# A recurrent layer with an ELU feed-forward block: the moment of the bank copies, the steps of the output sums, and the order of the last products

## The chip, the cores and the metric

The kernel runs on one core of a Trainium2 chip. The metric is the device time in microseconds (us) of one execution. The core's engines are named as in the profile: PE multiplies matrices (PEld are its weight loads), DVE, ACT and POOL work on vectors, SP issues transfers. PE writes to PSUM, which has eight banks here; DVE and ACT read PSUM and SBUF, POOL reads and writes SBUF alone.

## What is computed

The reference is a gated linear recurrence over 768 tokens for 4 x 8 heads of size 48, whose output goes through a feed-forward block with an ELU:

```python
f = 1.0 / (1.0 + np.exp(-f_logit))
for t in range(S):
    state = f[:, :, t, :, None] * state + np.einsum('bhd,bhe->bhde', k[:, :, t], v[:, :, t])
    y[:, :, t] = np.einsum('bhd,bhde->bhe', q[:, :, t], state)
...
h = x @ w_in
g = np.where(h > 0.0, h, alpha * (np.exp(np.minimum(h, 0.0)) - 1.0))
return (g @ w_out).astype(np.float32)
```

x has 3072 tokens of 384 numbers, w_in is 384 x 2048, w_out is 2048 x 384, all in fp32.

## The kernel before

The 3072 tokens are 12 units of 256. The program is one list written out by hand (`manual_schedule`): each engine does its instructions in the order in which the loop at L1263 emits them, so an instruction that waits holds up all that stands behind it on its engine. The loop runs over 16 half steps T for each unit. At an even T it emits the up-projection of one pair P, 256 of the 2048 hidden columns (`up`, for units from 1 on `up7`). At an odd T it emits the joins of that pair (`joined`), whatever `plan` has for this T, and the down-projection of an earlier pair (`down(P - LAG)`, two pairs behind). A unit has eight pairs, called P0 to P7 here.

Both projections save products by sums, as Strassen's method does. In `up7` (L946) PE makes four products in one PSUM bank (`pa`); ACT copies one of them to `u` (L963); DVE adds it to others (L965, `hh`); then `elu` of the pair before is emitted, and PE makes six products in a second bank (`pb`). In `joined` (L975) DVE adds the second bank's products to the first's in three instructions (L978), and ACT applies Relu and Exp (L988, L989). The two banks of tag `h` are taken in turn: the `pa` of a pair has to wait for L965 of the pair before, its `pb` for L978 of the pair before. `elu` (L1007) finishes the activation on DVE (L1010). After an even pair POOL makes four sums of hidden columns (SUMS_OF_TWO), after an odd one DVE makes three (SUMS_SOON) and POOL eight (SUMS_OF_FOUR).

In `down` two pairs, a quad, make 20 products of 128 x 128 x 128 (PRODUCTS, ten for the even pair and ten for the odd), each a row such as "x4 b10 c0": hidden column block or sum, weight block or combination of weights, target. The 16 targets c0 to c15 lie four to a bank in the banks m3, m0, m1 and m2, in this order; all four quads of a unit add into them. After the unit's last product `ended` (L1092) is called at once: ACT copies three banks to SBUF (`kept`, L1097) and c15 to a piece of `spare` (L1099), and the 22 output sums (OUTPUTS) with the stores go on a list, `pending`. c12 to c14 are read straight from PSUM, in the first three sums. Each half step takes four items off that list (SPREAD). The last product of a unit is emitted at step 3 of the next (T%16 = 3), so the list is empty after step 8.

Other work around this. At step 2 of a unit the keys of the next are transposed (PE and ACT). At step 5 `both` makes its state products (banks a0, a1) and its scores (banks m3 and m0 of the products), which DVE masks and adds up; at this step there is no down-projection, and step 7 has two. At steps 9 and 11 its outputs and the carried part follow. At steps 9, 11, 13 and 15 the decays of the unit after that are made: a scan (L680) and a reciprocal (L685) on DVE for three of them, products on POOL (L675). At step 13 POOL makes differences of x for the next unit (`blend`, L944). Weights are read again to be checked by ACT at steps 2, 6, 10 and 14 (L658, L659).

In the last unit the even pair of the last quad gives no products; all 20 are emitted together after the last up-projection, in the order of the banks, then the copies and OUTPUTS_AT_THE_END, of which POOL makes four sums and DVE 18.

```python
        if j == NP - 1:
            ended(m)
...
        for f in pending[:SPREAD]:
            f()
        del pending[:SPREAD]
```

Of the kernel before, what the change touches and what calls it, by code (L numbers as in the profile page):

```python
# [355 lines left out]
def table(text):  # L356
    return [tuple(row.split()) for row in text.split(",") if row.strip()]
# [6 lines left out]
    "a0 x0 - x1, a1 a0 - x4, a2 x5 + a1, a3 x0 - x4, "  # L364
)
SUMS_SOON = table(
    "a5 x2 - x6, a7 x4 + x2, a10 x2 - x7, "
)
SUMS_OF_FOUR = table(
    "a12 a0 + x7, a4 x6 - x7, a6 x5 + a4, a9 x4 + x6, a8 x1 + x2, a8 a8 - x3, a13 x0 + x2, a11 x3 - x7, "  # L370
)
COMBINATIONS = table(
    "b0 w3 - w4, b1 w0 + b0, b2 w1 - b1, b1 b1 - w2, b1 b1 - w10, b4 w11 + w8, b3 w7 - b2, b2 w10 _ b2, "
# [2 lines left out]
)  # L376
PRODUCTS = (
    table(
        "x4 b10 c0, x5 w5 c11, x1 b12 c14, a0 b1 c2, a1 b8 c1, a2 w3 c8, a3 b6 c7, x7 b9 c10, x2 b5 c4, "
        "a5 w6 c9, "  # L380
    ),
    table(
        "a7 b3 c3, a10 b4 c5, a12 b7 c6, a4 b13 c11, a6 b0 c15, a9 b11 c15, a8 w11 c14, a8 w10 c13, "
        "a13 b2 c13, a11 w9 c12, "
    ),
)
OUTPUTS = table(
    "o0 c7 + c12, o1 c3 - c13, o2 c7 - c14, c1 c0 + c1, c2 c2 - c1, c4 c3 - c4, c5 c5 + c4, c6 c6 - c2, "
    "c8 c8 - c6, c9 c9 - c5, o0 o0 + c10, o0 o0 + c5, o0 o0 - c6, o1 o1 + c7, o1 o1 + c2, o2 o2 + c4, "
    "o2 o2 - c1, o3 c10 + c8, o3 o3 - c9, o5 c11 - c0, o5 o5 - c9, o4 c8 - c15, "  # L390
)
OUTPUTS_AT_THE_END = table(
    "c1 c0 + c1, c2 c2 - c1, c4 c3 - c4, c5 c5 + c4, c6 c6 - c2, c8 c8 - c6, o0 c7 + c5, o1 c3 + c7, "
    "o2 c7 + c4, o5 c11 - c0, c9 c9 - c5, o3 c10 + c8, o0 o0 - c6, o1 o1 + c2, o2 o2 - c1, o5 o5 - c9, "
    "o3 o3 - c9, o0 o0 + c10, o2 o2 - c14, o1 o1 - c13, o4 c8 - c15, o0 o0 + c12, "
)


# [2 lines left out]
def fast(ctx: ExitStack, tc: tile.TileContext, q, k, v, f_logit, w_in, w_out, out, flag, outer):  # L401
# [18 lines left out]
    nc = tc.nc  # L420
# [9 lines left out]
    NU = B * UPB  # L430
# [4 lines left out]
    NP = NFT // 2  # L435
    DH = DM // 2
    NQ = NFT // 4
    DIRECT = 1
    PLAIN = 2
    SPREAD = 4  # L440
# [108 lines left out]
    spare = cst.tile([128, sum(sizes)], FP32, name="spare")  # L549
# [10 lines left out]
    wo = cst.tile([128, NFT, DM], FP32, name="wo")  # L560
# [414 lines left out]
    def joined(P):  # L975
        m, j = order[P]
        h, pb = phs[P]
        add = lambda to, x, y: nc.vector.tensor_tensor(out=to, in0=x, in1=y, op=ALU.add)  # L978
        u43 = sb.tile([128, 2, 128], FP32, tag="u43h", name=f"u43h{m}_{j}")
        add(u43[:], pb[:, 0::2], h[:, 0:1].broadcast_to([128, 2, 128]))  # L980
        add(h[:, 2:4], pb[:, 1::2], u43[:])
        add(h[:, 4], pb[:, 0], u43[:, 1])
        exped(P, h[:, 1:].rearrange("n (i t) f -> n i (t f)", i=2))
# [23 lines left out]
    def elu(P):  # L1007
        m, j = order[P]
        g = gs[P]
        nc.vector.scalar_tensor_tensor(  # L1010
            out=g[:], in0=g[:], scalar=-1.0, in1=phs.pop(P), op0=ALU.add, op1=ALU.max
        )
        if m < PLAIN:
            return
        Q = P // 2
        if P % 2 == 0:
            ss[Q] = sb.tile([128, 14, 128], FP32, tag="sums", name=f"sums{m}_{j // 2}")
        for engine, rows in ((nc.gpsimd, SUMS_OF_TWO),) if P % 2 == 0 else (
            (nc.vector, SUMS_SOON), (nc.gpsimd, SUMS_OF_FOUR)
        ):  # L1020
            for row in rows:
                combined(engine, lambda name: hidden(Q, name), row)

    def combined(engine, at, row):
        to, x, sign, y = row
        engine.tensor_tensor(out=at(to), in0=at(x), in1=at(y), op=ALU.add if sign == "+" else ALU.subtract)  # L1026

    def hidden(Q, name):
        i = int(name[1:])
        if name[0] == "a":  # L1030
            return ss[Q][:, i]
        t, f = divmod(i, 4)
        return gs[2 * Q + f // 2][:, f % 2, t * 128 : (t + 1) * 128]

    def weight(Q, name):
        i = int(name[1:])
        if name[0] == "b":
            return combos[i][:, Q]
        f, n = divmod(i, 3)
        return wo[:, 4 * Q + f, n * 128 : (n + 1) * 128]  # L1040

    left = []

    def down(P):
        m, j = order[P]
        if m < PLAIN:
            if j == 0:
                pms[m] = [
                    ps.tile([128, DM], FP32, tag=f"m{i}", name=f"psM{m}_{i}") for i in ((0, 3) if m else (1, 2))
                ]  # L1050
            pm, g = pms[m], gs.pop(P)
            for i in range(2):
                for t in range(NW):
                    nc.tensor.matmul(
                        pm[t][:], lhsT=g[:, i, t * 128 : (t + 1) * 128], rhs=wo[:, 2 * j + i, :],
                        start=(j == 0 and i == 0), stop=(j == NP - 1 and i == 1),
                    )
            if j == NP - 1:
                o = (outer if (NU - m) % 2 else sb).tile([128, 2, DM], FP32, tag="o", name=f"o{m}", bufs=1)
                for t in range(NW):  # L1060
                    nc.scalar.copy(o[:, t], pm[t][:])
                    t0 = m * U + t * 128
                    nc.sync.dma_start(out=out[t0 : t0 + 128, :], in_=o[:, t])
                del pms[m]
            return
        Q = P // 2
        if j == 0:
            pms[m] = [ps.tile([128, 4, 128], FP32, tag=f"m{i}", name=f"psM{m}_{i}") for i in (3, 0, 1, 2)]
            begun.clear()
        pm = pms[m]  # L1070
        whole = m == NU - 1 and j >= NP - 2
        if whole and j == NP - 2:
            return
        todo = PRODUCTS[j % 2]
        if whole:
            todo = sorted(PRODUCTS[0] + PRODUCTS[1], key=lambda row: int(row[2][1:]) // 4)
        for x, y, c in todo:
            bank, at = divmod(int(c[1:]), 4)
            nc.tensor.matmul(  # L1079
                pm[bank][:, at], lhsT=hidden(Q, x), rhs=weight(j // 2, y),  # L1080
                start=bank not in begun, stop=(j == NP - 1), skip_group_check=True,
            )
            begun.add(bank)
        if j % 2:
            gs.pop(P - 1), gs.pop(P), ss.pop(Q)
        if j == NP - 1:
            ended(m)

    begun = set()
    pending = []  # L1090

    def ended(m):  # L1092
        pm = pms.pop(m)
        o = (outer if (NU - m) % 2 else sb).tile([128, 2, DM], FP32, tag="o", name=f"o{m}", bufs=1)
        kept = sb.tile([128, 12, 128], FP32, tag="kept", name=f"kept{m}", bufs=1)
        for b in range(3):
            nc.scalar.copy(kept[:, 4 * b : 4 * b + 4], pm[b][:])  # L1097
        last = spare[:, NQ * 128 : (NQ + 1) * 128]
        nc.scalar.copy(last, pm[3][:, 3])  # L1099

        def at(name):
            i = int(name[1:])
            if name[0] == "o":
                return o[:, i // 3, i % 3 * 128 : (i % 3 + 1) * 128]
            return last if i == 15 else kept[:, i] if i < 12 else pm[3][:, i - 12]

        def store(*queues):
            for t in range(2):
                for h in ((1, 0) if t else (0, 1)):
                    queues[t].dma_start(  # L1110
                        out=out[m * U + t * 128 : m * U + (t + 1) * 128, h * DH : (h + 1) * DH],
                        in_=o[:, t, h * DH : (h + 1) * DH],
                    )

        if m < NU - 1:
            pending.extend(lambda row=row: combined(nc.vector, at, row) for row in OUTPUTS)
            pending.append(lambda: store(nc.sync, nc.sync))
            return
        for row in OUTPUTS_AT_THE_END:
            combined(nc.gpsimd if row[0] in ("o3", "o5") else nc.vector, at, row)  # L1120
        left.append(store)
# [141 lines left out]
    for T in range(NU * NFT):  # L1263
        P = T // 2
        sevens = order[P][0] >= DIRECT
        if T % 2 and sevens:
            joined(P)
        if T % 2 == 0 and P and order[P - 1][0] < DIRECT:
            elu(P - 1)
        for f in plan.pop(T, ()):  # L1270
            f()
        if T % 2 == 0:
            up(P)
        elif P >= LAG and T not in joint:
            if T - 2 in joint:
                down(P - LAG - 1)
            down(P - LAG)
        for n in later.pop(T, ()):
            split(n)
            if n not in (A1[2], A1[2] + 1):  # L1280
                lower(n)
        for f in pending[:SPREAD]:
            f()
        del pending[:SPREAD]
    elu(NU * NP - 1)
    for P in range(NU * NP - LAG, NU * NP):
        down(P)
# [50 lines left out]
```

## Time and profile before

| what | value |
|---|---|
| median of 3 runs | 628.16 us (626.54 to 630.26) |
| the profiled execution | 629.21 us, span 627.5 us |
| mean granted PE clock | 0.962 of full speed |
| PE, PEld busy | 91%, 82% |
| DVE, POOL, ACT busy | 73%, 61%, 44% |
| DMA | 54.37 MB, mean 87 GB/s |
| costliest DVE sums of L1026 | output and bank sums 128x128: 0.28 to 0.54 us each |

The span runs from the first to the last instruction; 1.7 us of the run's time lie around it. A line of the waits names the engine and line that waited, what it waited for, and then the sum in us, the number of times and the longest. A line of the timeline gives start and length in us, engine, line, operation, target and sources, and in brackets how long the engine had been idle before and what released it. Start times count from the span's start.

### The profile page before, as it was taken

The page shows a single profiled execution, that of the slowest core. Times are in us where ns is not written, and L with a number is a line of the kernel's source. Part 1 is how long each engine was busy: PE and PEld are TensorE (multiplying, and loading weights), DVE is VectorE, ACT ScalarE, POOL GpSimd, SP SyncE. Part 2 cuts the span into 40 slices and gives each one's busy share as a digit, 9 for nine tenths or more (in the row PEclk, how much of TensorE's full clock was granted, in tenths as well). Part 3 has the DMA queues.
Part 4 walks back from the last instruction along what each step waited for, and adds up shares of the span by engine and source line. Part 5 has one row for each costly group of instructions (what it writes and reads, how often), then busy time and mean ns, then how long its engine had stood idle before and what let it go on. Part 6 is the DMA issues. An engine that isn't in the chain of part 4 may idle for free. (4 is left out here: it accounts for less than half of the span.)

```text
span 627.5 us, 16865 instructions
## 1 busy us (share of the span) xinstructions
PE 568.0 (91%) x6778; PEld 516.7 (82%) x6778; DVE 460.5 (73%) x1006; ACT 277.3 (44%) x602; POOL 382.0 (61%) x715
## 2 busy tenths in 40 slices
PE   6798999999989979998997997997998899799892
PEld 3576778789989979987997996996997899799792
DVE  8879887667768858858858867775885884844864
ACT  3387833443343444443543443435444355245231
POOL 6502995685864864764783694585476477356453
PEclk9998999999999998997997997999999899899898
DMA  8999840230321341250170160143125013020001
GB/s 213 253 214 293 224 98 2 56 98 3 86 93 53 80 123 34 54 170 14 46 196 14 46 170 28 52 113 92 51 61 143 18 44 88 14 71 2 14 15 30
DMA packets 39192, 54.37 MB, mean 87 GB/s; under 512 B 4000, under 2 KB 28928, under 8 KB 39104
## 3 DMA queue, kind: packets, MB, share of 16 engines
q1 hardware_dynamic: 38304, 52.61, 32.2%
q8 instruction: 55, 0.90, 0.6%
q10 hardware_dynamic: 800, 0.59, 0.4%
q14 instruction: 33, 0.27, 0.1%
HBM read 45.02 MB, written 4.72 MB: 79 GB/s over the span
## 5 line engine op out<-in xcount | busy, mean ns | idle before, releaser
L956 PE MATMUL psH<-xt,wi 128*128 128x128 f32 (+1 forms) x1056 | 201.6, 301 | 2.5 <-DVE hh L965 2.5
L988 ACT ACTIVATE gg<-hh 128x512 f32<-128x512 f32 x88 | 55.5, 631 | 291.1 <-DVE hh L978 280.4
L956 PE MATMUL psH<-xt,area 128*128 128x128 f32 x704 | 128.4, 286 | 33.5 <-DVE hh L978 32.9
L956 PEld LDWEIGHTS psH<-xt,wi 128*128 128x128 f32 x1056 | 151.5, 197 | 5.8 <-DVE hh L965 3.4
L956 PEld LDWEIGHTS psH<-xt,area 128*128 128x128 f32 x704 | 110.8, 198 | 42.9 <-issue 29.1
L1026 POOL TENSOR_TENSOR sums<-sums,gg 128x128 f32<-128x128 f32 x120 | 62.2, 518 | 101.9 <-DVE gg L1010 95.7
L1026 POOL TENSOR_TENSOR sums<-gg 128x128 f32<-128x128 f32 x160 | 75.9, 474 | 73.5 <-DVE gg L1010 69.1
L1079 PE MATMUL psM<-area,sums 128*128 128x128 f32 x720 | 117.5, 282 | 1.2 <-DVE sums L1026 1.2
L965 DVE TENSOR_TENSOR hh<-psH,u 128x256 f32<-128x256 f32 x88 | 37.0, 420 | 107.7 <-ACT u L963 107.6
L1079 PEld LDWEIGHTS psM<-area,sums 128*128 128x128 f32 x720 | 99.2, 197 | 3.3 <-DVE sums L1026 1.4
L1079 PE MATMUL psM<-wo,sums 128*128 128x128 f32 x400 | 72.1, 278 | 0.0
L1010 DVE SCALAR_TENSOR_TENSOR gg<-gg,hh 128x512 f32<-128x512 f32 x88 | 63.1, 717 | 1.5 <-ACT gg L989 1.5
L685 DVE RECIPROCAL f<-f 128x256 f32<-128x256 f32 x36 | 62.8, 1748 | 1.1
L989 ACT ACTIVATE gg<-gg 128x512 f32<-128x512 f32 x96 | 60.5, 630 | 3.0
L1079 PE MATMUL psM<-area,gg 128*128 128x128 f32 x320 | 59.4, 289 | 0.6 <-DVE o L1026 0.5
L1079 PEld LDWEIGHTS psM<-wo,sums 128*128 128x128 f32 x400 | 58.1, 194 | 0.9
L1026 POOL TENSOR_TENSOR sums<-gg,gg 128x128 f32<-128x128 f32 x120 | 57.6, 493 | 0.0
L978 DVE TENSOR_TENSOR hh<-psH,u43h 128x256 f32<-128x256 f32 (+1 forms) x176 | 54.7, 353 | 3.0
L675 POOL TENSOR_TENSOR q<-q,f 128x256 f32<-128x256 f32 x48 | 37.1, 774 | 22.4 <-DMA f<-f 17.6
L1079 PEld LDWEIGHTS psM<-area,gg 128*128 128x128 f32 x320 | 48.1, 201 | 1.9 <-ACT u L963 0.7
L1026 POOL TENSOR_TENSOR sums<-gg,sums 128x128 f32<-128x128 f32 x80 | 43.6, 544 | 6.3
L675 POOL TENSOR_TENSOR k<-k,f 128x256 f32<-128x256 f32 x48 | 36.1, 754 | 15.6 <-DVE f L680 5.8
(113 smaller groups left out, 873.9 us busy)
## 6 DMA issues: line engine op xcount, KB each, us to landing
area<-in_moe_w_out_dram SPq DMA_DIRECT2D x8, 768.0 KB, 10.7
again<-in_moe_w_in_dram SPq DMA_DIRECT2D x16, 384.0 KB, 4.6
again<-in_moe_w_out_dram SPq DMA_DIRECT2D x16, 384.0 KB, 3.5
k<-in_k_dram SPq DMA_DIRECT2D x12, 384.0 KB, 4.5
q<-in_q_dram SPq DMA_DIRECT2D x12, 384.0 KB, 5.6
v<-in_v_dram SPq DMA_DIRECT2D x12, 384.0 KB, 5.8
area<-in_moe_w_in_dram SPq DMA_DIRECT2D x8, 576.0 KB, 9.0
out_dram<-o SPq DMA_DIRECT2D x38, 96.0 KB, 1.7
```

The source lines that it names most:

```text
L675: e.tensor_tensor(out=t[n][:, p], in0=t[n][:, p], in1=t["f"][:, p, "kq".index(n)], op=ALU.mult)
L685: nc.vector.reciprocal(f[:, p, 1], f[:, p, 0])
L956: nc.tensor.matmul(to, lhsT=lhs, rhs=rhs, start=(n == 0), stop=True, skip_group_check=True)
L965: add = lambda to, x, y: nc.vector.tensor_tensor(out=to, in0=x, in1=y, op=ALU.add)
L978: add = lambda to, x, y: nc.vector.tensor_tensor(out=to, in0=x, in1=y, op=ALU.add)
L988: nc.scalar.activation(g[:], h, AF.Relu, scale=-1.0)
L989: nc.scalar.activation(g[:], g[:], AF.Exp, scale=-1.0)
L1010: nc.vector.scalar_tensor_tensor(out=g[:], in0=g[:], scalar=-1.0, in1=phs.pop(P), op0=ALU.add, op1=ALU.max)
L1026: engine.tensor_tensor(out=at(to), in0=at(x), in1=at(y), op=ALU.add if sign == "+" else ALU.subtract)
L1079: nc.tensor.matmul(pm[bank][:, at], lhsT=hidden(Q, x), rhs=weight(j // 2, y), start=bank not in begun, stop=(j == NP - 1), skip_group_chec ...
```

## The change

Five things are edited.

- Away from the last unit, `ended` is no longer called with the last product, but put on a list `soon`, which the loop empties at the end of the next even half step, behind `up`.
- `ended` copies all four banks whole (the fourth to 512 columns of `spare`), so that every output sum reads SBUF. In the last unit three banks are copied, and the fourth is read from PSUM.
- `pending` is worked off at odd half steps only, and not at steps 3 and 5: four items each at steps 7, 9, 11, 13, 15 and 1 of the next unit, five in the last unit.
- Targets are numbered anew so that c0 to c7 (banks 0 and 1) get all their products from the even pair and c8 to c15 nearly all from the odd one. a7 takes the place of a5 in the even list; the soon sums are reordered so that a7 is made first; a13 goes ahead of a8 among POOL's. The two products of a8 with w10 and w11, which are neighbours in memory, become one that is 256 wide.
- In the last unit the first seven products of the last quad are emitted at its even pair, the others after the odd one, in the usual order and no longer sorted.

```diff
 SUMS_SOON = table(
-    "a5 x2 - x6, a7 x4 + x2, a10 x2 - x7, "
+    "a7 x4 + x2, a10 x2 - x7, a5 x2 - x6, "
 )
 SUMS_OF_FOUR = table(
-    "a12 a0 + x7, a4 x6 - x7, a6 x5 + a4, a9 x4 + x6, a8 x1 + x2, a8 a8 - x3, a13 x0 + x2, a11 x3 - x7, "
+    "a12 a0 + x7, a4 x6 - x7, a6 x5 + a4, a9 x4 + x6, a13 x0 + x2, a8 x1 + x2, a8 a8 - x3, a11 x3 - x7, "
 )
 PRODUCTS = (
     table(
-        "x4 b10 c0, x5 w5 c11, x1 b12 c14, a0 b1 c2, a1 b8 c1, a2 w3 c8, a3 b6 c7, x7 b9 c10, x2 b5 c4, "
-        "a5 w6 c9, "
+        "x4 b10 c0 1, x5 w5 c11 1, x1 b12 c14 1, a0 b1 c2 1, a1 b8 c1 1, a2 w3 c7 1, a3 b6 c3 1, x2 b5 c5 1, "
+        "x7 b9 c6 1, a7 b3 c4 1, "
     ),
     table(
-        "a7 b3 c3, a10 b4 c5, a12 b7 c6, a4 b13 c11, a6 b0 c15, a9 b11 c15, a8 w11 c14, a8 w10 c13, "
-        "a13 b2 c13, a11 w9 c12, "
+        "a10 b4 c8 1, a5 w6 c10 1, a12 b7 c9 1, a4 b13 c11 1, a9 b11 c15 1, a6 b0 c15 1, a13 b2 c13 1, "
+        "a8 w10 c13 2, a11 w9 c12 1, "
     ),
 )
...
-        whole = m == NU - 1 and j >= NP - 2
-        if whole and j == NP - 2:
-            return
         todo = PRODUCTS[j % 2]
-        if whole:
-            todo = sorted(PRODUCTS[0] + PRODUCTS[1], key=lambda row: int(row[2][1:]) // 4)
+        if m == NU - 1 and j >= NP - 2:
+            todo = PRODUCTS[0][:7] if j < NP - 1 else PRODUCTS[0][7:] + PRODUCTS[1]
...
-        if j == NP - 1:
+        if j == NP - 1 and m < NU - 1:
+            soon.append(lambda: ended(m))
+        elif j == NP - 1:
             ended(m)
...
-        for b in range(3):
-            nc.scalar.copy(kept[:, 4 * b : 4 * b + 4], pm[b][:])
-        last = spare[:, NQ * 128 : (NQ + 1) * 128]
-        nc.scalar.copy(last, pm[3][:, 3])
+        last = spare[:, NQ * 128 : (NQ + 4) * 128].rearrange("p (c f) -> p c f", c=4) if m < NU - 1 else pm[3]
+        for b in range(3 if m == NU - 1 else 4):
+            nc.scalar.copy(kept[:, 4 * b : 4 * b + 4] if b < 3 else last, pm[b][:])
...
-            return last if i == 15 else kept[:, i] if i < 12 else pm[3][:, i - 12]
+            return kept[:, i] if i < 12 else last[:, i - 12]
...
-        for f in pending[:SPREAD]:
-            f()
-        del pending[:SPREAD]
+        if T % 2 == 0:
+            while soon:
+                soon.pop()()
+        elif T % (2 * NP) not in (3, 5):
+            now = SPREAD + (P >= (NU - 1) * NP)
+            for f in pending[:now]:
+                f()
+            del pending[:now]
```

OUTPUTS and OUTPUTS_AT_THE_END have the same sums under the new numbers of the targets; the second list is also in another order.

## The prediction

> **What bounds the kernel now.** I read the page first: PE is busy 91% of the span, and its row of tenths dips once per unit. So I read the waits, then the timeline around one dip, then windows that cut a unit in two. "Step n" is half step T%16 = n; P0 to P7 are a unit's pairs (up-projection at step 2i, `joined` at 2i+1).
>
> ```profile
> PE psH L956 <- DVE hh L978: 32.9, 20, 3.4
> PEld psH L956 <- issue: 29.1, 9, 3.5
> DVE o L1026 <- ACT spare L1099: 27.3, 9, 3.0
> ```
>
> PE stands for 32.9 us until DVE frees the second up-projection bank (L978), and DVE stands nine times for 3.0 us at the head of its own queue because its first output sum (L1026) needs the last bank copy. The timeline of the unit at 528 shows how these belong together:
>
> ```profile
> 530.89 1.54 ACT L1097 COPY kept<-psM 128x512 f32<-128x512 f32 x3
> ...
> 532.47 0.30 ACT L963 COPY u<-psH 128x128 f32<-128x128 f32 x1
> 532.64 0.68 DVE L1026 TENSOR_TENSOR o<-kept,psM 128x128 f32<-128x128 f32 x3 [3.04 <-ACT spare L1099]
> 533.24 0.28 DVE L1026 TENSOR_TENSOR kept<-kept 128x128 f32<-128x128 f32 x1
> 533.44 0.42 DVE L965 TENSOR_TENSOR hh<-psH,u 128x256 f32<-128x256 f32 x1
> ...
> 535.63 1.66 DVE L1026 TENSOR_TENSOR kept<-kept 128x128 f32<-128x128 f32 x4
> ...
> 537.21 0.41 DVE L978 TENSOR_TENSOR u43h<-psH,hh 128x256 f32<-128x256 f32 x1
> ...
> 538.42 0.68 PE L956 MATMUL psH<-xt,area 128*128 128x128 f32 x4 [3.35 <-DVE hh L978]
> ```
>
> ACT copies the banks ahead of `u` for P2, DVE waits for them with `hh` queued behind, and four more sums stand between `hh` and the joins at 537.21 for which PE waits.
>
> ```profile
> 528.26:546.14 17.88, 13.74 (x210) 13.00 (x209) 13.95 (x42) 6.90 (x16) 7.63 (x16) 0.90 0.12 34
> 546.14:576.83 30.69, 30.69 (x370) 30.01 (x369) 15.45 (x39) 12.85 (x33) 17.30 (x38) 1.00 0.13 37
> 477.80:495.71 17.91, 13.77 (x211) 12.96 (x209) 14.46 (x44) 6.43 (x16) 7.63 (x16) 0.90 0.10 30
> 495.71:528.26 32.55, 32.15 (x376) 30.89 (x375) 23.61 (x47) 15.83 (x40) 23.72 (x45) 1.00 0.21 56
> ```
>
> Columns: length, then busy PE, PEld, DVE, ACT, POOL, then granted clock. Steps 4 to 7 (17.9 us) hold the idle PE and a clock of 0.90; steps 8 to 3 of the next unit are full of matmuls. The second pair of lines has a next unit's decays (DVE 23.61), the first has none (15.45). After the idle the clock is halved:
>
> ```profile
> 437.40:440.40 3.00, 3.00 (x12) 2.82 (x13) 2.47 (x7) 2.75 (x8) 0.07 (x1) 0.50 0.00 0
> ```
>
> **Part 1: copies half a step later, sums from step 7 on.** Walk with the durations of the unit at 528.26. Up to `exp` of P1 (ends 530.99) nothing changes, nor does PE's wait of 0.43 before 529.75. Then ACT takes `u` at 531.0 (before 532.47); `hh` 531.3, ELU of P1 (0.71) to 532.35, three soon sums (1.15) to 533.5, joins of P2 (1.07) to 534.57; before, they ended at 538.2. PE: second products of P2 end at 531.46, state products to 532.43, scores to 533.55. The scores' banks m3 and m0 are product banks 0 and 1, whose copies are the first two in ACT's queue: 531.27 + 2 x 0.51 + 0.08 = 532.37, just in time. First products of P3 end at 534.44, the second ones start at 534.65 instead of 538.42: 0.2 idle where 0.35 + 3.35 was. Down-projections of P0 and P1 (20 products, start to start 0.22 each, 4.4 us) follow the 1.54 us of second products: step 8 starts at 540.6. The mask and state work of DVE (1.3 + 1.5) lies beside them. So the stretch takes 540.6 - 528.26 = 12.34 us instead of 17.88.
>
> The half clock is in this: seven PE waits of 3.35 us each begin a stretch at 0.50. The Trainium skill ("TensorE: Matmul & The Clock Gate", Part 1) says that the gate throttles after at least one idle window of about 3.4 us and that the window runs free; by that rule none of these waits is long enough. The trace has it after waits of 3.35, and once after 2.05 (586.5 to 590.6: 0.59), but not after 2.08 (184 to 190: 1.00). By the rule alone I would gain 3.5 us per unit, by the row 5.5; I take the row, and no half clock for the waits of at most 1 us that I leave (the trace has 0.91 at 199.18 without one).
>
> **Part 2: what the moved sums do to steps 8 to 3.** Before, 20 of the 23 items are done by step 7; now four at 7, 9, 11, 13, 15 and two plus the stores at step 1. Steps 9, 11 and 13 also have DVE's scan and reciprocal (0.845 + 1.75). Behind the sums stand `hh`, ELU and soon sums of the next pair, on which PE's down-projection depends (x2, x7 and a7 stand last there, 1.54 us in), and the next joins, on which the second up bank depends. What a sum costs:
>
> ```profile
> L1026 DVE TENSOR_TENSOR o<-kept,psM 128x128 f32<-128x128 f32 x27 | 6.1, 283 | 27.3 <-ACT spare L1099 27.3
> L1026 DVE TENSOR_TENSOR o<-kept 128x128 f32<-128x128 f32 x21 | 6.0, 294 | 0.0
> ...
> L1026 DVE TENSOR_TENSOR o<-kept,spare 128x128 f32<-128x128 f32 x10 | 5.1, 514 | 0.0
> ```
>
> A sum is 0.28 alone and about 0.54 when POOL works beside it; the one with a PSUM operand is 0.28 always. This is what the skill's "SBUF — State Buffer" (Who interferes with whom) says: a DVE instruction with two SBUF inputs and a GpSimd one that reads SBUF exclude each other. It speaks against reading all sums from SBUF: all contended, four take 2.1 us; all free, 1.15 (the x4 groups in the timeline: 1.15 and 1.66). From POOL's rows in the unit at 495.71 I take 1.2 at steps 9 and 11 (POOL between groups), 1.9 at 13 (its blend, 2.8 us, overlaps), 1.6 at 15.
>
> Walk from step 8 = 0, in before's order: joins of P4 end at 5.44 (0.66 earlier, two sums gone), scan and reciprocal to 8.13, sums to 9.35, `hh` of P5 just after (9.25 before). Joins of P5 to 11.3, decays 13.9, sums 15.1; `hh` of P6 then (14.64 before); ELU ends 16.15 where PE wants x2 at 15.9: 0.3 lost. Joins of P6 to 18.3 where PE wants its bank at 17.8: 0.55. Decays 20.85, sums 22.75; joins of P7 24.85, check 25.4, sums 27.0. PE starts the next unit at 22.1, waits about 1.0 for `hh` of P7 and 0.85 for its joins; then down and transposes bring step 2 to 29.4. Before it came at 27.88, with a wait of 0.40 in it. Net loss 1.5 us (0.8 with all sums free, 3.0 with all contended). Work late by 1.5 is caught up by step 2, where before shows DVE 3.8 us idle. POOL's sums of four start with the ELU, and its last is still ahead of PE's last product.
>
> Per unit with decays: 12.34 + 32.55 + 1.5 = 46.4 against a mean of 50.47 ((538.42 - 235.58)/6): 4.1 us.
>
> **Small parts.** a8 as one 256-wide product: at 530.27 a 128-wide and a 256-wide product take 0.65 to the next group, so 256 costs 0.43 = 2 x 0.22: nothing, its weight load being hidden. Between -0.02 and +0.02 each, under 1 us over 40; I take 0. The fourth copy: 0.59 for 0.29 on ACT, beside PE's scores; queued behind it is `relu` of P2, which waits for the joins (534.57) anyway, while the copies are over at 533.4; without that cover 0.3 per unit. Bank labels, soon sums and stores (SP's queue, 0.34 per issue) move with no one behind them that is late: 0; without cover, 0.2 for one soon sum.
>
> **Sum.** Six units with decays: 6 x 4.1 = 24.4. The unit at 177 (wait 2.08 + 0.33, decays after): 2.4 - 1.0 = 1.4. The unit at 528 has no decays: 5.5. The last (576.83 to 591.84): joins of P2 end at 582.55 instead of 586.3, wait 2.05 and half clock (1.7) go, with bank 3's copy at 581.45 in time for third product: 3.9; its fives of sums fit, DVE being half idle. The tail: seven products go ahead of the last ELU, but POOL's last sum (616.2) still sets PE's end, 616.55 for 617.08, and DVE's 18 sums (5.9 us) start at 613.4 instead of 614.16, longer contended: 0.5. Total 35.7. The profiled run was 629.21 (span 627.5, 1.7 around it) and becomes 593.5; on the median, 1.05 lower, 592.5.
>
> **Rivals.**
> 1. The sums run free of POOL: loss 0.8 instead of 1.5, some waits shorter: 6 x 0.7 + 1: 587. For: POOL idles 0.27 of that stretch. Against: 340 ns mean already.
> 2. The scores wait for all four copies, not two (one wait on ACT's last): 533.4 for 532.43, 0.8 per unit over seven: 598. For: `both` takes two banks at once, and copies come back to back. Against: banks are separate tiles, and at 580.50 PE waits for single copies.
> 3. The sums all meet POOL, which in turn slows: loss 3.0 to 4, 602 to 607. For: soon sums, issued beside POOL, do take 0.54.
> 4. Slower: DVE becomes the bound between steps 8 and 1. It has 23.61 us there and gets 16 sums more; at 0.54 that is 32.3, and with its waits for `u` (about 6 us in that stretch) 38.5, a loss of 6; if PE's waits then bunch into two half-clock windows, 3.4 more. 9.4 per unit over seven units is 65.8 against 45.7 gained elsewhere: 648. It decides above a loss of 6.5 per unit. Against: `u` waits and sums overlap in queue order.
> 5. It does not do what it says: DVE's wait for copies is only moved to step 7. Against: copies end at 533.4 and the first sum starts near 539.7. Then nothing: 628.
>
> **Numbers.** Mine 0.57 (588 to 598), rival 1 0.14, 2 0.09, 3 0.13, 4 0.04, 5 0.03. Range 583 to 605 leaves out 4, 5 and the far ends. A measurement tells about 0.5% (3 us) from nothing: faster 0.93, same 0.03, slower 0.04.
>
> **What would show it.** Right: DVE's wait on a copy gone; PE's waits of 3.35 gone, waits of 0.3 to 1 at steps 12 to 0 instead; stretch of steps 4 to 7 near 12.3 at clock 1.00; unit period near 46.4; DVE over 85% busy in steps 8 to 3. Wrong: half clock left in steps 12 to 2, PE waiting on a copy before the scores, contended sums throughout, or a POOL sum of four that comes late.

## The result and the profile after

The changed kernel takes 586.29 us in the median (585.78 to 589.72, four runs) against 629.11 of the kernel before beside it: a ratio of 0.933, with an interval of 0.928 to 0.938. Predicted were 592.5, range 583 to 605, with 588 to 598 as its own stretch (chance 0.57); the measured time lies inside the range and just under that stretch. The profiled execution was 589.72 us with a span of 588.0. Two of the page's rows after, PE's busy tenths and its granted clock:

```profile
PE   6789989999999999999999999999999999999993
...
PEclk9999989999999999999999999999999999999997
```

The dip once per unit and the lower clock there are gone. The waits of the same profile, with the sum in us, the number and the longest:

```profile
DVE hh L965 <- ACT u L963: 88.8, 45, 4.2
...
PE psH L956 <- DVE hh L978: 7.3, 14, 0.5
```

PE waits 7.3 us for the joins instead of 32.9, and never more than 0.5. DVE's wait for the last bank copy does not appear any more. The timeline at a unit's end (P2 starts at 500.50) reads like this now; a bracket would show a wait of the instruction:

```profile
503.32 0.25 ACT L963 COPY u<-psH 128x128 f32<-128x128 f32 x1
...
503.47 1.56 ACT L1098 COPY kept<-psM 128x512 f32<-128x512 f32 x3
...
503.60 0.42 DVE L965 TENSOR_TENSOR hh<-psH,u 128x256 f32<-128x256 f32 x1 [1.57 <-ACT u L963]
...
504.86 1.13 PE L763 MATMUL psS<-q,k 64*64 64x64 f32 x64
...
505.81 0.41 DVE L978 TENSOR_TENSOR u43h<-psH,hh 128x256 f32<-128x256 f32 x1
...
507.02 0.68 PE L956 MATMUL psH<-xt,area 128*128 128x128 f32 x4
```

`u` is copied ahead of the banks, the joins start 5.3 us after P2 instead of 8.95, and PE goes on to the second products of P3 without waiting. The scores follow the state products at once, at 504.86, before the third of the copies has ended (505.03): two copies are enough for them. The two stretches of a unit (length, then busy PE, PEld, DVE, ACT, POOL, clock), first without a next unit's decays, then with them:

```profile
500.50:513.09 12.59, 12.07 (x206) 11.46 (x207) 10.26 (x26) 7.23 (x16) 7.34 (x16) 1.00 0.23 67
513.09:543.67 30.58, 30.58 (x365) 29.75 (x363) 22.07 (x57) 12.85 (x33) 18.05 (x38) 1.00 0.11 31
454.44:467.04 12.60, 12.07 (x206) 11.46 (x207) 10.75 (x28) 7.11 (x16) 7.33 (x16) 1.00 0.24 67
467.04:500.50 33.46, 32.57 (x371) 30.75 (x369) 28.02 (x62) 15.49 (x40) 24.53 (x46) 1.00 0.19 46
```

Steps 4 to 7 went from 17.9 to 12.6 us in these two units; steps 8 to 3 are longer by about one us where there are decays (32.55 before), and DVE is busy 28.0 of 33.5 us there.

### The profile page after: what moved, and what is told of

Its sections match the earlier page's. It is cut to its first block, busy times and chain, and to the rows that moved or that the text cites. A ratio compares the mean times of both kernels' runs of the same rounds, so it can differ in the third digit from the quotient of the medians.

```text
span 588.0 us, 16718 instructions
## 1 busy us (share of the span) xinstructions
PE 554.5 (94%) x6698; PEld 499.7 (85%) x6698; DVE 467.8 (80%) x1006; ACT 279.7 (48%) x601; POOL 385.9 (66%) x715
## 5 line engine op out<-in xcount | busy, mean ns | idle before, releaser
L956 PE MATMUL psH<-xt,wi 128*128 128x128 f32 (+1 forms) x1056 | 197.2, 296 | 1.9 <-DVE hh L965 0.6
L956 PEld LDWEIGHTS psH<-xt,wi 128*128 128x128 f32 x1056 | 147.0, 192 | 7.2 <-DVE hh L965 4.3
L956 PE MATMUL psH<-xt,area 128*128 128x128 f32 x704 | 124.3, 279 | 9.4 <-DVE hh L978 7.3
L956 PEld LDWEIGHTS psH<-xt,area 128*128 128x128 f32 x704 | 106.7, 192 | 18.8 <-PE psH L956 10.0
L1026 POOL TENSOR_TENSOR sums<-gg 128x128 f32<-128x128 f32 x160 | 79.6, 498 | 59.3 <-DVE gg L1010 51.1
L965 DVE TENSOR_TENSOR hh<-psH,u 128x256 f32<-128x256 f32 x88 | 36.8, 418 | 89.0 <-ACT u L963 88.8
L1026 POOL TENSOR_TENSOR sums<-sums,gg 128x128 f32<-128x128 f32 x120 | 58.8, 490 | 72.4 <-DVE gg L1010 66.1
L1077 PE MATMUL psM<-wo,sums 128*128 128x128 f32 (+1 forms) x320 | 64.0, 302 | 0.6 <-POOL sums L1026 0.6
L1026 POOL TENSOR_TENSOR sums<-gg,gg 128x128 f32<-128x128 f32 x120 | 58.3, 514 | 0.0
L1077 PE MATMUL psM<-area,gg 128*128 128x128 f32 x320 | 56.6, 279 | 0.0
L1077 PEld LDWEIGHTS psM<-wo,sums 128*128 128x128 f32 x320 | 51.5, 191 | 3.2 <-POOL sums L1026 1.0
L675 POOL TENSOR_TENSOR q<-q,f 128x256 f32<-128x256 f32 x48 | 36.6, 764 | 18.4 <-DMA area<-in_moe_w_in_dram 15.5
L1077 PEld LDWEIGHTS psM<-area,gg 128*128 128x128 f32 x320 | 45.3, 192 | 0.9 <-ACT spare L1098 0.2
L1026 POOL TENSOR_TENSOR sums<-gg,sums 128x128 f32<-128x128 f32 x80 | 41.4, 517 | 6.3
```

The costliest lines, as they stand in the source:

```text
L675: e.tensor_tensor(out=t[n][:, p], in0=t[n][:, p], in1=t["f"][:, p, "kq".index(n)], op=ALU.mult)
L956: nc.tensor.matmul(to, lhsT=lhs, rhs=rhs, start=(n == 0), stop=True, skip_group_check=True)
L1077: nc.tensor.matmul(pm[bank][:, at : at + count], lhsT=hidden(Q, x), rhs=weight(j // 2, y, count), start=bank not in begun, stop=(j == NP - ...
```

## The experiments

For each kernel I give two lengths from its profile, means over the six units 4 to 9 (the unit whose up-projection runs): A from the first product of P2 to that of P4, B from P4 to P2 of the next unit. Before: A 18.39, B 32.09. Changed kernel: A 12.60, B 33.43. In the kernel before A differs between units (17.7 to 19.2), because the half clock lasts 3.4 us in units 4 and 8 to 10 and 6.8 us in units 5 to 7 (granted clock 0.50 from 283.4 to 290.2, for one). The runs were made in three groups, each with its own runs of the kernel before: 629.24 us beside e1, e2, e3 and e5, 628.25 beside e4, e6, e7 and e9, 627.34 beside e8, e10 and e11. A ratio is always to these.

**Only the copies later (e1).**

```diff
-        elif T % (2 * NP) not in (3, 5):
-            now = SPREAD + (P >= (NU - 1) * NP)
-            for f in pending[:now]:
-                f()
-            del pending[:now]
+        for f in pending[:SPREAD]:
+            f()
+        del pending[:SPREAD]
```

> The copies stand behind u as in the changed kernel, but the output sums start at step 4, four in every half step. Theory (DVE's wait behind ACT's copies was the loss; where the sums stand costs about the same everywhere): four sums stand ahead of the joins of P2 again, 1.2 to 1.7 us, so steps 4 to 7 take about 14.1 us instead of 12.6, but steps 8 to 3 go back from 33.4 to about 32; period about 46, no half clock, time 583 to 591. Rival (the steps of the sums were the loss): PE's wait at step 6 stays near 2.5 to 3 us with half clock behind it, time above 605.

615.76 us, ratio 0.981 (0.976 to 0.985). A is 14.0, as expected, but B is 35.4, not 32: that it costs about the same wherever the sums stand was wrong. The timeline, where DVE works off step 8, shows why:

```profile
491.39 0.28 DVE L1026 TENSOR_TENSOR o<-o,kept 128x128 f32<-128x128 f32 x1
...
491.59 0.54 DVE L1026 TENSOR_TENSOR o<-kept 128x128 f32<-128x128 f32 x1
...
491.75 0.61 PE L956 MATMUL psH<-xt,wi 128*128 128x128 f32 x4
...
492.17 0.43 DVE L1026 TENSOR_TENSOR o<-o,kept 128x128 f32<-128x128 f32 x1
492.52 0.54 DVE L1026 TENSOR_TENSOR o<-kept 128x128 f32<-128x128 f32 x1
492.98 0.41 DVE L978 TENSOR_TENSOR u43h<-psH,hh 128x256 f32<-128x256 f32 x1
...
494.19 0.68 PE L956 MATMUL psH<-xt,area 128*128 128x128 f32 x4 [1.84 <-DVE hh L978]
```

Four sums of an even half step stand between DVE's soon sums and the joins, and PE waits 1.84 us for these joins. At an odd half step the same sums stand behind the joins, ahead of `hh`, which has to wait for `u` anyway. It is not that B holds more of the sums: ten of a unit's 22 start in it here (3.4 us of DVE), 18 in the changed kernel (7.1 us).

**Only the sums later (e2).**

```diff
-        if j == NP - 1 and m < NU - 1:
-            soon.append(lambda: ended(m))
-        elif j == NP - 1:
+        if j == NP - 1:
             ended(m)
```

> The output sums stand at steps 7 to 1 as in the changed kernel, but ACT copies the four banks at once at step 3, ahead of u of P2. Theory: u comes 2.1 us later, so do the joins of P2, and PE waits about 2.3 us for them at step 6; steps 4 to 7 take about 14.7 us, without half clock, period 48; over eight unit ends about 16 us more than the changed kernel: 598 to 606. Rival (the steps of the sums were the loss, the copies' place costs nothing because DVE no longer waits for a copy): 585 to 590.

602.88 us, ratio 0.961 (0.956 to 0.966), A 14.53, B 33.43. As expected: the copies ahead of `u` cost about 2 us per unit, all of it in A. PE's waits for the joins, 7.3 us in the changed kernel and 32.9 before, are

```profile
PE psH L956 <- DVE hh L978: 20.4, 23, 1.8
```

Against the kernel before, e1 is worth 13.5 us and e2 26.4; together they would be 39.9, and the change gave 42.8. So both parts are needed and roughly add up, and the larger share is that of the sums' steps.

**The even half steps by themselves (e10).** The sums at the steps 8, 10, 12, 14, 0 and 2, each half a step later than in the changed kernel. This kernel leaves out the last two sums and the stores of unit 10.

```diff
-        elif T % (2 * NP) not in (3, 5):
+        if T % 2 == 0 and T % (2 * NP) not in (4, 6):
```

> The changed kernel with the four sums at even half steps (8, 10, 12, 14, 0, 2) in place of odd ones (7 to 1). The same number of sums in the same stretch; only now they stand ahead of the joins, not behind them. Theory (what cost e1 its time is that in even half steps a sum stands between the soon sums and the joins for which PE waits): steps 8 to 3 take 36 us or more, 604 to 618. Rival (only the amount of DVE work in the stretch counts): 584 to 590.

642.28 us, ratio 1.023 (1.019 to 1.026): slower than before, with B at 39.1. The direction is that of the theory, the size is more than I gave it. B holds 20 of the 22 sums instead of 18, and they take 8.9 us of DVE instead of 7.1; these 1.8 us are too little for the 5.7 by which B grew. With e1, where B has fewer sums than in the changed kernel and is longer, this shows that the place counts and not the amount of DVE work alone. PE's waits for the joins sum to 41.4 us here, to 7.3 in the changed kernel. The half clock comes back in four of the six units, and B is the same with it (39.26 in unit 8) and without it (39.11 in unit 9). In its timeline DVE stands still for `u` and does the sums then, while PE waits:

```profile
413.13 0.42 DVE L965 TENSOR_TENSOR hh<-psH,u 128x256 f32<-128x256 f32 x1 [0.79 <-ACT u L963]
...
415.32 0.74 DVE L1026 TENSOR_TENSOR kept<-kept 128x128 f32<-128x128 f32 x2
...
415.99 1.00 DVE L1026 TENSOR_TENSOR o<-o,kept 128x128 f32<-128x128 f32 x2
416.91 0.41 DVE L978 TENSOR_TENSOR u43h<-psH,hh 128x256 f32<-128x256 f32 x1
...
418.12 0.68 PE L956 MATMUL psH<-xt,area 128*128 128x128 f32 x4 [2.09 <-DVE hh L978]
```

DVE's whole wait for `u` is 132.8 us here, 117.7 in e1, 107.6 before, 88.8 in the changed kernel. This fits sums that fill the wait when they stand ahead of `hh`; which of them do was not measured one by one.

**Sums from step 5 on (e11).**

```diff
-        elif T % (2 * NP) not in (3, 5):
+        elif T % (2 * NP) != 3:
```

> The changed kernel with sums at step 5 too, so four each at 5, 7, 9, 11, 13 and two at 15. They stand behind the joins, masks and state work of step 5, and the second products of P3 have been let go by then. Theory: steps 4 to 7 stay at 12.6 us, step 1 is freed, 582 to 587. Rival (any sum in steps 3 to 6 brings PE's wait back): 595 or more.

589.2 us, ratio 0.938 (0.934 to 0.941); A 12.64, B 33.8. That sums behind the joins of step 5 do not bring PE's wait back is confirmed; the small gain that I expected from a freed step 1 is not there. B rose by 0.4: in four of the six units PE now waits 0.50 us for the joins at step 14 too (at 440.36, for one), where the changed kernel does not wait. What makes these joins late stays open.

**The old tables (e3)**: products, soon sums and POOL's sums as before, in the changed kernel.

```diff
-    "a7 x4 + x2, a10 x2 - x7, a5 x2 - x6, "
+    "a5 x2 - x6, a7 x4 + x2, a10 x2 - x7, "
...
-        "a10 b4 c8 1, a5 w6 c10 1, a12 b7 c9 1, a4 b13 c11 1, a9 b11 c15 1, a6 b0 c15 1, a13 b2 c13 1, "
-        "a8 w10 c13 2, a11 w9 c12 1, "
+        "a7 b3 c3 1, a10 b4 c5 1, a12 b7 c6 1, a4 b13 c11 1, a6 b0 c15 1, a9 b11 c15 1, a8 w11 c14 1, a8 w10 c13 1, "
+        "a13 b2 c13 1, a11 w9 c12 1, "
```

> The changed kernel with the old products (a8 as two, a5 in the even list, old bank labels), old soon sums and old order of POOL's sums. Theory: a 256-wide product costs two 128-wide ones and the labels move nothing that is late: within 2 us of the changed kernel, 585 to 589. Rival (the merged product saves its weight load, or the products' order saves waits for sums): 590 to 596.

586.81 us, ratio 0.933 (0.928 to 0.938), the same as the changed kernel (A 12.61, B 33.22). The merged product and the new numbers are worth nothing that can be measured.

**Three sums from PSUM (e4).**

```diff
-        for b in range(3 if m == NU - 1 else 4):
-            nc.scalar.copy(kept[:, 4 * b : 4 * b + 4] if b < 3 else last, pm[b][:])
+        for b in range(3):
+            nc.scalar.copy(kept[:, 4 * b : 4 * b + 4], pm[b][:])
+        if m < NU - 1:
+            nc.scalar.copy(last[:, 3], pm[3][:, 3])
...
-            return kept[:, i] if i < 12 else last[:, i - 12]
+            return kept[:, i] if i < 12 else last[:, 3] if i == 15 and m < NU - 1 else pm[3][:, i - 12]
...
-        elif T % (2 * NP) not in (3, 5):
-            now = SPREAD + (P >= (NU - 1) * NP)
+        elif T % (2 * NP) != 3:
+            now = 3 if T % (2 * NP) == 5 else SPREAD + (P >= (NU - 1) * NP)
```

> The changed kernel, but c12 to c14 are read straight from PSUM again: ACT copies three banks and c15 alone, and the first three sums go to step 5, behind masks and state work, since the bank must be free for the products of step 7. Theory: a bank held by DVE's queue is a risk to PE; here the three sums (0.85 us, never contended) end near the first product into that bank, PE waits 0 to 1 us per unit, and three contended sums less give back about 0.4: 584 to 593. Rival (reading PSUM is as good or better, the move to SBUF costs contention only): 580 to 584.

591.99 us, ratio 0.941 (0.938 to 0.943). Its waits have a new line:

```profile
PE psM L1077 <- DVE o L1026: 8.4, 8, 1.5
```

A is 13.8, 1.2 more, because PE waits for the bank that DVE still reads; B is 32.5, 0.9 less. So per unit most of the loss comes back, and of the 5.7 us by which the median is longer some 2 lie in the last unit (its A is 12.55 instead of 10.51). Reading SBUF is not quicker: the three sums take 0.28 us each from PSUM (in e4), and 0.41 on average from SBUF (in the changed kernel). What SBUF gives is that the bank is let go. How much that is worth by itself is not shown, since the sums' steps changed too: e11, whose sums also start at step 5 and read SBUF, has 46.46 us for A and B together, e4 46.34. To keep these three sums at step 7 as well was not tried: there they would wait behind the products that need their bank.

**Matmuls in PE's wait, in the kernel before (e5, e9).** Six (e5) and three (e9) products of the identity into the bank m1; the edit shown is that of e9, e5 has `warm(6, "m1")`.

```diff
+        if m > 2 and m < NU - 1 and j == 3:
+            warm(3, "m1")
         products(
             (pb[:, 0], t[0], x[:, 1]), (pb[:, 2], t[2], x[:, 7]), (pb[:, 3], a[1][1], x[:, 9]),
```

> The kernel before, with six 128x512 products of the identity into the free bank m1 between the first and the second products of P3, in units 3 to 10, where PE stands 3.35 us. Their result is not used. They take about 2.6 us and end before DVE's joins, so the wait itself stays. Theory (the half clock behind the wait is a loss of its own, 1.7 to 2.8 us per unit): clock 1.00 in steps 6 to 8, 12 to 17 us faster than before, 612 to 617. Rival (the half clock is hidden by the DVE work that follows): 627 to 630. If they end too late, slower than before.

> The kernel before with three identity products of 128x512 in PE's wait, instead of six, which took 5.3 us and outlasted the wait: these take about 2.65 us and end inside it. Their result is not used. Theory (half clock is a loss of its own): clock 1.00, steps 4 to 7 take about 16.2 us instead of 17.9 to 19.2, seven or eight units, 610 to 617. Rival (the loss is given back by DVE's work that follows): 625 to 630.

e5: 627.04, ratio 0.997 (0.995 to 1.000). Inconclusive: the six took 5.3 us, outlasted the wait and held PE up. e9: 624.58, ratio 0.994 (0.992 to 0.997). Three took 2.74 and ended inside the wait; the clock stays at 1.00, and A is 16.2 instead of 18.4. But B is 34.0 instead of 32.1. The two stretches of unit 9 in e9 (these windows begin 0.3 us after P2), A of unit 10, and PE's waits for the joins in unit 9:

```profile
476.50:492.70 16.20, 14.65 (x216) 12.38 (x216) 12.79 (x39) 5.65 (x14) 6.89 (x15) 1.00 0.08 25
492.70:526.60 33.90, 32.40 (x374) 30.79 (x373) 24.88 (x51) 16.65 (x41) 24.41 (x47) 1.00 0.21 57
526.64:542.88 16.24, 14.69 (x217) 12.41 (x215) 12.90 (x39) 5.65 (x14) 7.42 (x16) 1.00 0.12 33
```

```profile
486.36 0.68 PE L956 MATMUL psH<-xt,area 128*128 128x128 f32 x4 [0.78 <-DVE hh L980]
500.42 0.68 PE L956 MATMUL psH<-xt,area 128*128 128x128 f32 x4 [0.91 <-DVE hh L980]
512.14 0.68 PE L956 MATMUL psH<-xt,area 128*128 128x128 f32 x4 [0.50 <-DVE hh L980]
```

The first of these waits is the rest of the old one and lies in A; the other two lie in B. PE wins 2.2 us by its clock and loses 1.9 of them in the next 34 us, mostly waiting for DVE, whose queue has not become shorter: in unit 9 PE stands 1.50 us in B where it stood 0.40. The rival was right for the units with decays: alone, the half clock was worth 0.3 us per unit there. Unit 10, whose next unit has no decays, is the counter-case: its A becomes 1.6 us shorter (17.88 to 16.24), and its B stays as it is (30.69 and 30.75). So the half clock is hidden where DVE has much to do behind it, and costs 1.6 us in this one unit, where it has not.

**Better steps for the sums (e6)**, **the checks behind `u` (e7)**, and **both (e8)**. The edit of e6, then that of e7:

```diff
-        elif T % (2 * NP) not in (3, 5):
-            now = SPREAD + (P >= (NU - 1) * NP)
+        else:
+            now = {7: 8, 9: 3, 11: 3, 13: 0, 15: 3, 1: 6}.get(T % (2 * NP), 0)
+            if P >= (NU - 1) * NP:
+                now = SPREAD + 1 if T % (2 * NP) > 5 else now
```

```diff
-        at_step(t + 4, lambda n=n: check(n))
+        checks[t + 4] = n
...
+        if T in checks:
+            check(checks[T])
         for n in later.pop(T, ()):
```

> The changed kernel with the sums where DVE waits for u in its profile: eight at step 7, three at 9, 11 and 15, none at 13, the rest with the stores at 1; the last unit as it is. Theory (in steps 8 to 3 the sums behind the decays make PE late): that stretch goes from 33.4 to about 32.2 us, seven units, 577 to 581. Rival (POOL's load sets that stretch): 584 to 588.

> The changed kernel with ACT's two checks of the reread weights (1.5 us, steps 2, 6, 10, 14) emitted behind u instead of ahead of it. Theory (PE's 0.5 before the second products of P2, which the change left, comes from these checks ahead of u of P1): that wait and the 0.15 before it go, steps 4 to 7 take 12.0 us, 579 to 583. Rival (u is late because of the copies of the keys alone): 586 to 588.

> The sums at the steps of e6 and the checks behind u of e7 together. Theory (the two took away different waits: DVE's late work in steps 8 to 3, and ACT's in steps 2 to 4): steps 4 to 7 take 11.8 us, steps 8 to 3 about 31.5, eleven nearly all pure matmul time; 566 to 570, under both. Rival (they take away the same waits): 573 to 576.

e6: 574.33, ratio 0.913 (0.911 to 0.915), A 12.42, B 31.87: more than expected. Eight sums fit at step 7, where DVE waits for `u` of P4 behind ACT's gates: they run from 409.19 to 411.74, and `u` starts at 412.17. PE then runs steps 8 to 15 without a wait for the joins. e7: 577.03, ratio 0.917 (0.915 to 0.920), A 11.85, B 33.0: the wait of 0.52 before the second products of P2 came from the checks, as supposed, since A has no wait of PE any more, and B gained 0.4 besides. e8: 567.48, ratio 0.904 (0.901 to 0.907), A 11.56, B 32.1; the joins are no longer among the things for which PE waits, and DVE's wait for `u` is down to

```profile
DVE hh L965 <- ACT u L963: 64.9, 33, 4.2
```

e8 is faster than both kernels of the change and than e6 and e7: it is 18.8 us under the changed kernel, where e6 is 12.0 and e7 9.3 under it, so most of the two gains adds up.

## Why the prediction was right

The prediction had the direction and the mechanism right, and the time within 1.1%: it was 6.2 us too slow. The measured 586.29 lies nearer to the 587 of rival 1 than to 592.5, but that is chance: what rival 1 assumes, sums that run free of POOL, did not happen (see the cost of a sum below). Both profiled runs can be set side by side by the start of PE's products. Up to P2 of unit 1 they do the same work, and the changed kernel's profiled run, the slowest of its four, was 2.55 us later there. From that point on:

| term | predicted gain | measured |
|---|---|---|
| six units with decays, 4 to 9 | 24.4 | 26.6 |
| unit 3 | 1.4 | 3.6 |
| unit 10 | 5.5 | 5.4 |
| unit 11 up to P4 | 3.9 | 4.6 |
| tail | 0.5 | 1.7 |
| sum | 35.7 | 42.0 |

- **Steps 4 to 7.** Predicted 12.34, measured 12.59: the order `u`, `hh`, ELU, joins came as walked, the joins' end 6.4 us after the start of P2 where the walk had 6.3, and no second wait of 0.2. Rival 2, scores waiting for all four copies, is out.
- **Steps 8 to 3.** Predicted 34.05, measured 33.43, 0.6 less: the loss is 1.34 on the mean of the six units (32.09), where I had 1.5 on one unit's 32.55. Most of the error comes from resting on that one unit. With steps 4 to 7, which took 0.26 more than predicted, it makes 0.4 us per unit, the 2.2 between 24.4 and 26.6. DVE's busy share is 28.0 of 33.5, 84%, a little under the 85% foretold. Of the loss 1.2 us lie in steps 0 to 3, about where the walk had it (1.3). There PE waits 0.13 for `hh` of P7 and 0.52 for its joins, where I had 1.0 and 0.85; the waits of 0.3 and 0.55 at steps 12 and 14 are not there.
- **Unit 3.** I charged it 1.0 for its sums, and steps 8 to 3 became 1.3 shorter (34.22 to 32.92). This is the other large error. Before, two sums of step 8 stood ahead of the joins for which PE waits:

```profile
197.30 0.28 DVE L1026 TENSOR_TENSOR o<-o,kept 128x128 f32<-128x128 f32 x1
...
197.50 0.54 DVE L1026 TENSOR_TENSOR o<-kept,spare 128x128 f32<-128x128 f32 x1
...
197.97 0.41 DVE L978 TENSOR_TENSOR u43h<-psH,hh 128x256 f32<-128x256 f32 x1
...
199.18 0.68 PE L956 MATMUL psH<-xt,area 128*128 128x128 f32 x4 [0.91 <-DVE hh L978]
```

  This wait and a later one of 0.50 (at 210.90, with no output sum just ahead of its joins) are gone. Both are those of e9 in B: unit 3 is the one of these units that has no half clock before step 8, and e9 takes the half clock from the others.
- **The cost of a sum.** That a sum with both operands in SBUF takes longer beside POOL held, against rival 1; and not all of them met POOL, against rival 3. The 51 output sums of the changed kernel beside which POOL did nothing took 276 to 293 ns, the 161 that ran beside it 443 on average. Groups of L1026 after:

```profile
L1026 DVE TENSOR_TENSOR o<-o,kept 128x128 f32<-128x128 f32 x85 | 34.2, 419 | 1.1
...
L1026 DVE TENSOR_TENSOR kept<-kept 128x128 f32<-128x128 f32 x70 | 23.7, 371 | 0.4
...
L1026 DVE TENSOR_TENSOR o<-kept,spare 128x128 f32<-128x128 f32 x36 | 14.2, 434 | 0.0
```

  o with kept went from 329 to 419 ns, and the three sums that had a PSUM operand from 283 to 406 (they are 27 of the 36 in the last group; the others are the sum with c15). In the unit at 454.44 four took 1.1, 1.2, 1.4 and 2.1 us at steps 9, 11, 13 and 15, 5.8 in all, where I had 1.2, 1.2, 1.9 and 1.6, 5.9 in all: the sum was right, the shares only roughly.
- **The half clock.** It went, as predicted. But I wrote that of 5.5 us per unit two came from the clock. In the sum this did no harm, since A was walked as a whole; as a cause it was wrong for the six units with decays: e9 takes the half clock away alone and gets 0.3 us per unit. What the clock took there, DVE's queue would have taken. Only in unit 10 does e9 keep 1.6 us. The gain of the change is that of the order in DVE's and ACT's queues, and the clock recovers with it. That seven waits each bring one half clock was also too simple: in units 5 to 7 it lasted 6.8 us and began inside the wait (at 283.4, with the wait ending at 285.25).
- **Rival 4**, slower than before, is what e10 measures (642.28), but by the place of the sums ahead of the joins and not by their amount: DVE's sums in steps 8 to 3 took 1.8 us more there, and the stretch 5.7. The prediction saw the joins' place ("two sums gone") and credited 0.66 for it, without seeing that this decides.
- **Small parts.** They were put at nothing, and e3 confirms it for the tables: the merged product, the numbers of the targets and the order of the sums. The fourth copy and the stores were not tested by themselves.
- **The tail.** From the start of the last pair to the end of DVE's last sum it went from 13.75 to 13.4 us, 0.4 where 0.5 was predicted; the other 1.3 us lie behind that, in the last stores (7.4 to 6.1 us). They are the same stores, in a changed order of the last sums, and I don't assign this to the change.

## What to carry to other kernels

Work that nobody waits for has a good place in an in-order queue: behind the instruction that frees another engine, and ahead of one that has to wait for its own input anyway; the same sums half a step later, ahead of the next such instruction, made this kernel slower than it had been. Read for each waiting engine what stands ahead of its releaser, on every engine of the chain: here putting the copies back ahead of `u` on ACT costs 17 us (e2), the sums back at every half step 29 us (e1), and moving the checks gains another 9 (e7). A lower clock behind a wait looks like a loss to add, but may only hide the next wait; the way to know is to keep the clock up and change nothing else.

## What was not expected of the hardware

Keeping the clock full through the wait (e9) moved A from 18.4 to 16.2 and B from 32.1 to 34.0: a half clock of 3.4 to 6.8 us per unit was nearly free where DVE had decays and sums to do behind it, and cost 1.6 us in the unit without decays.

Three 128x512 products in fp32 take 2.74 us. They are six instructions in the profile: each fp32 product is two, and as a 128-wide one costs 0.22 us from start to start, one of 512 should take four times as much. I had counted half of that in e5.

In e10 PE's second products ran slower (1.03 for the group that takes 0.82) just after a wait of 2.09, with one of 0.98 shortly before:

```profile
414.20 0.71 PE L1077 MATMUL psM<-area,gg 128*128 128x128 f32 x4 [0.98 <-DVE gg L1010]
```

The granted clock was 0.68 from 418.10 to 421.00. Two units later the same two waits, 0.98 at 518.57 and 2.09 at 522.49, were followed by a clock of 1.00 (522.5 to 525.9). So in this kernel the length of a wait alone does not tell whether the half clock comes.
